# Attention start of a fused block: maxima 12 tiles ahead instead of 11, head 0 finished in front of head 1's maxima, and the stacks of the first nine heads dealt anew

## The chip, the cores and the metric

One Trainium2 chip, one core. The metric is the device time of one execution of the whole kernel in microseconds; three runs of the kernel before gave a median of 968.77 us (965.73 to 971.95).

## The reference, cut to what matters

32 heads of attention (4 batches of 8), then two gated feed-forward blocks. Only the attention part, the first third of the time, is touched.

```python
q_rot, k_rot = rotate(q), rotate(k)          # x*cos + swapped(x)*sin
scores = scale * q_rot @ k_rot.T             # 576 x 576 per head, 64 deep
scores = scores - max(scores, axis=-1)
attn = exp(scores) / (sum(exp(scores)) + 1e-9)
out = attn @ v
```

## The kernel before

Numbers are fp32, and TensorE takes a rounded form of it (fp32r); so each operand is cut into a high part and a rest, and the two are stacked in the 128 rows of one tile. **K1**, **Q1**, **K2**, **Q2** are these stacks of a head (five buffers each, so head h uses buffer h mod 5). A head has five tiles of 128 keys or queries (the last has 64).

The work of a head h goes through these stages:

- **load(h)** brings the 576 KB of q and k and of their swapped halves into `raw` (four buffers).
- **rope(h)**: three products and sums of 128 x 576 on GpSimd (POOL), for the first heads partly on VectorE (DVE).
- **stacks**: `high` is a copy on ScalarE (ACT) of the rotated rows into K1, and two copies by DMA from K1[64:] into Q1[:64] and Q2; `low` is a subtraction on POOL into K2 and two copies by DMA, K2 into Q1[64:] and K1[:64] into K1[64:]. This last one overwrites what the two copies of `high` read, so it waits for both to land. All four are issued on the queue of SyncE (SP), which is in order. `first_stacks` makes the same with ACT and DVE alone, without DMA.
- **maxima** (`row_max`, tiles `sm`): a query tile against all keys with K1 and Q1, and a DVE reduction into a column of `MX`. When the five columns of a head are there, TensorE transposes them, DVE copies them to `mt`, and a DMA on ACT's queue writes them as a row into Q2. So the subtraction of the maximum is one more row of the second pair of matmuls of `scores`.
- **scores** (tiles `st`): K1 x Q1, then K2 x Q2 with that row, then exp on ACT into `pc` (for the fifth tile `pt` and `ph`, and a subtraction on DVE).
- **values** (tiles `pv`): attn times v, 3 tiles behind the scores; the fifth tile takes `VS`, the stacks of v.

The main loop counts **ticks** t: tick t holds scores of tile t mod 5 of head t // 5. Maxima of head m, tile c are taken at tick 5m + c - AHEAD, 11 ticks ahead of that tile's scores, after a ramp at the start. Everything else is put into a table by tick (`later`), for most heads by LEAD: the rope's three steps 26, 25 and 23 ticks ahead of tick 5h, `high` 20, `low` 17, the row of -1 in K2 11. A tick is a place in the order, not a time: each engine runs its own instructions in the order in which they were written and waits for data alone. From tick 15 on, eleven chunks of weights (`raw64`, `t64`) are loaded and converted beside this, one every ten ticks, each with two operations on ACT, four on DVE and one on POOL.

The start before: `warm` matmuls on zeros while head 0 is loaded; the maxima of head 0 (tick -9) and its row (`first_row`); then the maxima of head 1 with idle matmuls between them; then tick 0.

Of the kernel before, what the change touches and what calls it, by code (L numbers as in the profile page):

```python
# [8 lines left out]
F32 = mybir.dt.float32  # L9
# [3 lines left out]
AF = mybir.ActivationFunctionType  # L13
# [29 lines left out]

INVERSE = 5, 7, 8, 11, (24, 26)

MATRIX, APART, CONVERT, ROWS = 15, 10, 15, (151, 159)


IDLE = 17, 2, 5, 0, 2, 5, 6, 1, 0, 1


@with_exitstack
def tile_kernel(ctx: ExitStack, tc: tile.TileContext, qk, vv, tabs, w_in, g_ln, wsgT, b_sg, w_out, u_r, v_r, w1, w2, out):
    nc = tc.nc
# [31 lines left out]
    D = 64  # L86
# [65 lines left out]

    def stacks(h, ticks):

        rot = RAW[h % NR][:, 0]
        K1, Q1, K2, Q2 = (t[h % NS] for t in (K1s, Q1s, K2s, Q2s))
        a, z = slice(0, D), slice(D, P)

        def high():
            nc.scalar.activation(K1, rot, AF.Copy)
            nc.sync.dma_start(f(Q1[a]), f(K1[z]))
            nc.sync.dma_start(f(Q2[a, 0:S]), f(K1[z]))

# [4 lines left out]
        if h < len(BY_ACT):  # L170
            steps = rope(nc.gpsimd, h) + first_stacks(h)
        else:
            steps = rope(nc.gpsimd, h) + (high, low, lambda: nc.sync.dma_start(f(K2[D:D + 1]), less_one))
            value_stacks(h)
        for tick, fn in zip(ticks, steps):
            later(tick, fn)

    def value_stacks(h):
        VS = VSs[h % 4]
        src = VVs[(h // 2) % 3][:, SPLIT, h % 2, :D]  # L180
        later(max(NC * h - SPLIT_V[0], SPLIT_V_FIRST[0]), lambda: nc.scalar.activation(VS[:, 0, :, :D], src, AF.Copy))
        later(max(NC * h - SPLIT_V[1], SPLIT_V_FIRST[1]), lambda: (nc.gpsimd if h > 1 else nc.vector).tensor_tensor(VS[:, 1, :, :D], src, f(VS[:, 0, :, :D]), ALU.subtract))

    def first_stacks(h):

        rot = RAW[h % NR][:, 0]
# [3 lines left out]
        def copy(on_act, out, x):  # L190
            if on_act:
                nc.scalar.activation(out, x, AF.Copy)
            else:
                nc.vector.tensor_copy(out, x)

        def high():
            e = BY_ACT[h]
            copy(e[0], Q1[z], rot[z])
            copy(e[1], Q1[a], rot[z])
            copy(e[2], K1[a], rot[a])  # L200
            copy(e[3], K1[z], rot[a])
            copy(e[4], Q2[a, 0:S], rot[z])

        def low():
            nc.vector.tensor_tensor(Q1[z], rot[z], f(Q1[z]), ALU.subtract)
            nc.vector.tensor_tensor(K2[a], rot[a], f(K1[a]), ALU.subtract)
        value_stacks(h)
        return high, low

    def row_max(h, t, done, tick):  # L210

# [25 lines left out]

# [135 lines left out]
    def later(t, fn):  # L373
        due.setdefault(t, []).append(fn)
# [24 lines left out]
    for fn in rope(nc.vector, 1)[:1] + rope(nc.gpsimd, 1)[1:]:
        later(T0, fn)  # L400
    for h in range(2):
        for tick, fn in zip(FIRST[h], first_stacks(h)):
            later(tick, fn)
# [23 lines left out]
    def warm(i):

        if i == 0:
            ps = psp.tile([P, 2, 512], F32, tag="ss", name="warm", bufs=3)[:, 0]  # L430
        elif IDLE[i]:
            ps = psp.tile([P, 2, 512], F32, tag="pv", name="warm", bufs=1)[:, 1]
        for _ in range(IDLE[i]):
            nc.tensor.matmul(ps, idle[:, :P], idle, start=True, stop=True)

    warm(0)
    n_max, last = 0, {}
    for t in range(T0, NC * NH + LAG):
        v = divmod(t - LAG, NC)
        if t >= LAG and v[1] == NC - 1:  # L440
            values(*v, t)
        if 0 <= t < NC * NH:
            if t < 3:
                warm(7 + t)
            scores(*divmod(t, NC))
        lo = lows[:-1] if 0 <= t < NC * NH and t % NC in SPLITS else lows[:]
        for fn in lo:
            fn()
        del lows[:len(lo)]
        if t >= LAG and v[1] == 0:  # L450
            values(*v, t)
        upto = 0 if t < -9 else NC if t < MAX_1 else max(2 * NC, min(t + AHEAD + 1, 2 * NC + RAMP * (t - RAMP_FROM) // 10, NC * NH))
        ready = [m for m, due_at in last.items() if due_at <= t]
        while n_max < upto or ready:
            m, c = divmod(n_max, NC) if n_max < upto else (NH, 0)
            done = ready.pop(0) if ready else None
            last.pop(done, None)
            if done == 0:
                warm(1)
                first_row()  # L460
                continue
            if m == 1:
                warm(2 + c)
# [453 lines left out]
```

## Time and profile before

| what | value |
|---|---|
| median of three runs | 968.77 us |
| the profiled execution's own time | 971.01 us |
| its span, first to last instruction | 969.2 us |
| attention, end of the last values | about 326 us |
| TensorE busy over the span | 96% |
| mean granted TensorE clock | 0.989 |

The span is the profiler's, the time is the device's for the same execution: 1.8 us lie outside the span. The median lies 2.2 us under that execution. Start and length of a row are in us; PE is TensorE, PEld its weight loads, SPq and ACTq the DMA queues of SP and ACT. A tick takes 1.7 us where TensorE never waits.

### The profile page before, as it was taken

The numbers are of one execution on the slowest core, as the hardware profiler recorded it, in microseconds if no ns is written. First come the engines' busy times: TensorE is split into PE (matmuls) and PEld (weight loads), VectorE is DVE, ScalarE is ACT, GpSimd is POOL, SyncE is SP. The second block draws the span as 40 slices with busy tenths as digits, with TensorE's granted clock in tenths as the row PEclk, the third lists the DMA queues.
The fourth block names the chain that finished last, engine by engine and source line by source line (L and its number), as shares of the span: only waits on it lengthen the run. The fifth ranks groups of instructions, "written<-read, shape, count | busy, mean of one in ns | idle before, by whom it ended". The sixth has DMA issues, their size and how long they took to land.

```text
span 969.2 us, 13195 instructions
## 1 busy us (share of the span) xinstructions
PE 930.1 (96%) x5180; PEld 783.9 (81%) x5180; DVE 534.9 (55%) x721; ACT 345.0 (36%) x550; POOL 387.9 (40%) x323
## 2 busy tenths in 40 slices
PE   6899999989989999999999899999999999999998
PEld 3587777767777798999999787888888888888887
DVE  7767878888775487443426945752652452222222
ACT  4366665556656553312315432321321230001000
POOL 7677887878751486242325542210210210000000
PEclk7899999999999999999999999999999999999999
DMA  5578677777651230000003001220230110000112
GB/s 176 141 189 207 174 176 181 192 169 190 151 139 33 72 123 1 2 1 1 23 23 109 22 22 36 95 88 1 69 106 1 57 53 0 1 1 22 44 45 86
DMA packets 58079, 78.00 MB, mean 80 GB/s; under 512 B 30505, under 2 KB 33860, under 8 KB 58018
## 3 DMA queue, kind: packets, MB, share of 16 engines
q1 hardware_dynamic: 57708, 77.08, 29.4%
q8 instruction: 41, 0.67, 0.3%
q14 instruction: 20, 0.16, 0.1%
q10 hardware_dynamic: 310, 0.08, 0.0%
HBM read 55.09 MB, written 4.79 MB: 62 GB/s over the span
## 4 chain that ended last, share of the span: by engine, by line
PE 73%; DVE 13%; DMA 9%; issue 2%; POOL 1%; ACT 1%; SPq 0%; DVEq 0%; POOLq 0%; ACTq 0%
PE a L544 20%; PE r L544 20%; PE pv L273 9%; DMA Q<-mt 6%; PE st L245 6%; PE w L544 5%; PE m L544 3%; PE sm L216 3%; PE u L544 3%; PE v L544 3%; DVE MX L221 2%; DVE ph L256 2%; DVE t L74 1%; DVE t L75 1%; DMA g<-in_wsgT 1%
## 5 line engine op out<-in xcount | busy, mean ns | idle before, releaser
L221 DVE TENSOR_REDUCE MX<-sm 128x1 f32<-128x576 f32 (+1 forms) x160 | 119.7, 751 | 58.9 <-PE sm L216 50.1
L273 PE MATMUL pv<-pc,VV 128*65 128x288 f32 x512 | 144.7, 405 | 0.5 <-DVE sums L294 0.5
L245 PE MATMUL st<-Q,K 65*128 65x288 f32 (+3 forms) x640 | 128.6, 321 | 15.6 <-DMA Q<-mt 13.9
L245 PEld LDWEIGHTS st<-Q,K 65*128 65x128 f32 (+3 forms) x640 | 96.0, 179 | 31.5 <-DMA Q<-mt 16.2
L737 DVE SCALAR_TENSOR_TENSOR RL<-r,RH 128x1024 fp32r<-128x1024 f32 (+1 forms) x38 | 42.3, 1112 | 123.8 <-ACT RH L736 123.7
L736 ACT ACTIVATE RH<-r 128x1024 fp32r<-128x1024 f32 (+1 forms) x38 | 35.6, 936 | 207.2 <-PE r L544 207.2
L248 ACT ACTIVATE pc<-st 128x576 f32<-128x576 f32 x128 | 81.8, 646 | 49.3 <-PE st L245 44.7
L752 DVE TENSOR_TENSOR X<-a,X 128x256 f32<-128x256 f32 (+4 forms) x65 | 46.4, 745 | 90.7 <-PE a L544 90.6
L544 PE MATMUL a<-RH,setB 128*128 128x512 f32 (+1 forms) x320 | 93.3, 368 | 0.0
L273 PEld LDWEIGHTS pv<-pc,VV 128*65 128x65 f32 x512 | 68.2, 137 | 29.6 <-DVE sums L294 0.7
L216 PE MATMUL sm<-K,Q 128*128 128x288 f32 (+1 forms) x320 | 77.3, 326 | 10.8 <-DVE MX L221 5.0
L544 PE MATMUL a<-RH,setA 128*128 128x512 f32 (+1 forms) x288 | 83.5, 366 | 0.0
L544 PE MATMUL r<-UH,setB 128*128 128x512 f32 (+1 forms) x256 | 73.2, 363 | 0.0
L544 PE MATMUL r<-UH,setA 128*128 128x512 f32 (+1 forms) x256 | 72.9, 363 | 0.1
L216 PEld LDWEIGHTS sm<-K,Q 128*128 128x128 f32 (+1 forms) x320 | 51.3, 184 | 20.2 <-DVE MX L221 6.3
L544 PEld LDWEIGHTS a<-RH,setB 128*128 128x128 f32 x320 | 58.2, 189 | 10.0
L148 POOL TENSOR_TENSOR raw<-raw,tab 128x576 f32<-128x576 f32 x30 | 45.9, 1530 | 43.4 <-DMA raw<-in_qk 43.4
L508 POOL TENSOR_TENSOR setB<-t,setB 128x512 fp32r<-128x512 f32 x16 | 20.7, 1295 | 102.9 <-ACT setB L697 91.8
L544 PEld LDWEIGHTS a<-RH,setA 128*128 128x128 f32 x288 | 52.1, 188 | 9.2
L544 PE MATMUL a<-RL,setB 128*128 128x512 f32 (+1 forms) x160 | 58.9, 368 | 0.0
L149 POOL TENSOR_TENSOR raw<-raw,tab 128x576 f32<-128x576 f32 x31 | 53.2, 1716 | 5.0 <-DMA raw<-in_qk 5.0
L544 PE MATMUL a<-RL,setA 128*128 128x512 f32 (+1 forms) x144 | 52.9, 368 | 0.0
(169 smaller groups left out, 1972.2 us busy)
## 6 DMA issues: line engine op xcount, KB each, us to landing
raw<-in_qk SPq DMA_DIRECT2D x31, 576.0 KB
Q<-K SPq DMA_DIRECT2D x87, 144.0 KB
raw<-in_w SPq DMA_DIRECT2D x24, 512.0 KB
VV<-in_vv SPq DMA_DIRECT2D x32, 160.0 KB
rb<-rr SPq DMA_DIRECT2D x15, 288.0 KB
K<-K SPq DMA_DIRECT2D x29, 144.0 KB
raw<-in_w_in SPq DMA_DIRECT2D x8, 512.0 KB
gt<-in_w SPq DMA_DIRECT2D x8, 512.0 KB
```

What stands on the lines that cost most here:

```text
L148: lambda: e.tensor_tensor(raw[:, 0], raw[:, 0], tab[:, 0], ALU.mult),
L149: lambda: e.tensor_tensor(raw[:, 1], raw[:, 1], tab[:, 1], ALU.mult),
L216: nc.tensor.matmul(ps[:TS[t], n, :HALF], Q1[:, t * P:t * P + TS[t]], K1[:, n * HALF:(n + 1) * HALF], start=True, stop=True)
L221: nc.vector.tensor_reduce(MXs[h % 2][:TS[t], t:t + 1], ps[:TS[t], :, :HALF], AX.XY, ALU.max)
L245: nc.tensor.matmul(ps[:kk, n, :HALF], l[:, c * P:c * P + kk], r[:, ns], start=st, stop=not st)
L248: nc.scalar.activation(h2(pc[:kk]), ps[:kk, :, :HALF], AF.Exp, scale=0.125)
L273: nc.tensor.matmul(o, l, r, start=(c == 0 and j == 0), stop=(c == NC - 1 and j == len(pr) - 1))
L508: return nc.gpsimd.tensor_tensor(out, a, b, ALU.subtract)
L544: nc.tensor.matmul(o, l, rr, start=(j == 0), stop=(j == n - 1))
L736: nc.scalar.activation(RH[:, s], ps[:, :, :WIDE[blk]], AF.Relu)
L737: nc.vector.scalar_tensor_tensor(RL[:, s], ps[:, :, :WIDE[blk]], 0.0, f(RH[:, s]), ALU.max, ALU.subtract)
L752: nc.vector.tensor_tensor(X[b][:, e2, xs], ps[:, :n, us], X[b][:, e2, xs], ALU.add)
```

## The change

- AHEAD is 12 instead of 11: in the steady part every maximum is written one tick earlier, and so is the row by its transpose and its DMA. The other steps of heads 11 to 31 keep their ticks.
- At the start, `first_head` puts head 0's row together piece by piece between its maxima. The scores of head 0 then come at once, and the maxima of head 1 between them (`MAXIMA` says how many maxima are written by each tick: 5 up to tick 1, 10 at tick 4, 15 at tick 7, 40 at tick 27). The values of head 0 are brought forward, and head 1's row is put together like head 0's at tick 5.
- Three heads instead of five get their stacks from ACT and DVE (`early_stacks`); head 2's with two copies by DMA. Heads 3 to 10 have ticks of their own (`LEADS`, six steps as in LEAD), and the loads of heads 4 to 12 (`LOADS`).
- The row's DMA of heads 2 to 5 comes one tick after the transpose's tick, which is now one after the last maximum, not two (`ROW`).
- Idle matmuls: 22 at the start instead of 17, ten of 384 columns between head 0's maxima, none later.

```diff
-LEAD_IN = (-20, -19, -19, -8, -8, 1), (-19, -18, -16, -3, -1, 4), (-3, -3, 0, 2, 4, 8)
+LEADS = {3: (4, 5, 6, 7, 8, 11), 4: (8, 9, 10, 11, 12, 15), 5: (12, 13, 14, 15, 16, 19), 6: (16, 17, 18, 19, 19, 23),
+         7: (19, 20, 21, 22, 22, 26), 8: (22, 23, 24, 25, 25, 29), 9: (25, 26, 27, 28, 29, 34), 10: (28, 29, 30, 31, 33, 39)}
+LOADS = {4: -8, 5: 3, 6: 6, 7: 8, 8: 12, 9: 16, 10: 19, 11: 22, 12: 25}
...
-AHEAD, RAMP_FROM, RAMP, MAX_1, ROW, ROW_0, ROW_1 = 11, -1, 25, -1, 2, -8, -9
+AHEAD, ROW = 12, (1, 2)
...
+        if h < 2:
+            return q + [dve(K1[a], rot[a]), act(K1[z], rot[a]), *lows, act(Q2[a, 0:S], rot[z])]
+        return q + [act(K1[a], rot[a]), send(K1[z], K1[a]), send(Q2[a, 0:S], Q1[a]), *lows]
...
+    def row_piece(h, ps, t):
+        nc.tensor.matmul(ps[:1, t // 4, t % 4 * P:(t % 4 + 1) * P], MXs[h][:, t:t + 1], ident, start=True, stop=True)
+        if t == 3:
+            nc.scalar.activation(Q2s[h][D:D + 1, :4 * P], ps[:1, 0, :4 * P], AF.Copy)
+        if t == 4:
+            nc.vector.tensor_copy(Q2s[h][D:D + 1, 4 * P:], ps[:1, 1, :P])
+
+    def first_head():
+        ps = psp.tile([P, 2, 512], F32, tag="pv", name="first_row", bufs=1)
         for t in range(NC):
+            row_max(0, t, None, 0)
+            if t > 1:
+                row_piece(0, ps, t - 2)
+            for _ in range(IDLE[1]):
+                nc.tensor.matmul(ps[:, 1, P:], idle[:, :P], idle[:, P:], start=True, stop=True)
+        for t in (NC - 2, NC - 1):
+            row_piece(0, ps, t)
...
+    early = {3: [(0, 0)], 4: [(0, 1), (0, 2)]}
...
+        if t == NC:
+            low_parts(len(lows))
+            values(0, 3, t)
+            ps = psp.tile([P, 2, 512], F32, tag="ss", name="second_row", bufs=3)
+            for c in range(NC):
+                row_piece(1, ps, c)
+            values(0, 4, t)
...
-        upto = 0 if t < -9 else NC if t < MAX_1 else max(2 * NC, min(t + AHEAD + 1, 2 * NC + RAMP * (t - RAMP_FROM) // 10, NC * NH))
+        upto = NC if t < 0 else min(MAXIMA.get(t, NC * NH), t + AHEAD + 1, NC * NH)
```

**Place 1, ACT's order, head 6.** Before, the copy that begins head 6's stacks (K1 buffer 1 from raw buffer 2) stands behind the exp of head 2's first tile; the numbers behind a name's first underscore are head or buffer, and tile:

```order
L248 ACTIVATE pc2_0_501<-st2_0_496 128x576
L162 ACTIVATE K1_1_96<-raw2_91 128x576
L248 ACTIVATE pc2_1_523<-st2_1_518 128x576
L226 DMA Q2_3_113<-mt4_509 1x5x128
L289 ACTIVATE stage1_536<-pv1_465 65x576
```

Now it stands behind the last tile of head 3, nine ticks later:

```order
L252 ACTIVATE pt3_631<-st3_4_626 64x576
L254 ACTIVATE ph3_633<-pt3_631 64x576
L182 ACTIVATE VS_1_121<-VV_2_119 128x64
L165 ACTIVATE K1_1_96<-raw2_91 128x576
L248 ACTIVATE pc4_0_664<-st4_0_659 128x576
```

So `high` of head 6 moved from tick 10 to tick 19, and `low` on POOL with it from tick 13 to tick 19.

**Place 2, TensorE's order, from the last scores of head 3 to the first maxima of head 6.** Before, the first maxima of head 6 follow head 3's last scores, nine ticks behind the copy of place 1:

```order
L245 MATMUL st3_4_663<-Q1_3_103,K1_3_98 64x288 x2
L245 MATMUL st3_4_663<-Q2_3_113,K2_3_108 64x288 x2
L216 MATMUL sm6_0_672<-K1_1_96,Q1_1_101 128x288 x2
L273 MATMUL pv3_653<-pc3_1_618,VV_1_118 65x288 x2
L245 MATMUL st4_0_686<-Q1_4_104,K1_4_99 128x288 x2
```

Now they come two ticks later, but that copy stands at the top of this piece, behind st3_4:

```order
L245 MATMUL st3_4_626<-Q2_3_113,K2_3_108 64x288 x2
L206 MATMUL sm5_2_635<-K1_0_95,Q1_0_100 128x288 x2
L206 MATMUL sm5_3_639<-K1_0_95,Q1_0_100 128x288 x2
L273 MATMUL pv3_613<-pc3_1_570,VV_1_118 65x288 x2
L245 MATMUL st4_0_659<-Q1_4_104,K1_4_99 128x288 x2
L245 MATMUL st4_0_659<-Q2_4_114,K2_4_109 128x288 x2
L206 MATMUL sm5_4_667<-K1_0_95,Q1_0_100 64x288 x2
L273 MATMUL pv3_613<-pc3_2_598,VV_1_118 65x288 x2
L245 MATMUL st4_1_675<-Q1_4_104,K1_4_99 128x288 x2
L245 MATMUL st4_1_675<-Q2_4_114,K2_4_109 128x288 x2
L206 MATMUL sm6_0_682<-K1_1_96,Q1_1_101 128x288 x2
```

Between the copy and the first use stood nine ticks of TensorE's work; nine pairs of matmuls stand there now.

**Place 3, DVE's order in the steady part, at the row of head 13** (`mt13`). Before, the row's copy stands behind the subtraction for `ph` of head 10 and one maximum:

```order
L256 TENSOR_TENSOR ph10_1368<-pt10_1366,ph10_1368 64x576
L221 TENSOR_REDUCE MX_1_116<-sm13_1_1390 128x1
L224 CAST mt13_1395<-sm13_1_1390 5x128
L221 TENSOR_REDUCE MX_1_116<-sm13_2_1412 128x1
L325 TENSOR_TENSOR X0_66<-stage4_823,rb2_1158 64x576
```

Now it stands in front of that subtraction and of the last step of a conversion:

```order
L77 SCALAR_TENSOR_TENSOR t64_175<-raw64_174,t64_175 128x512
L211 TENSOR_REDUCE MX_1_116<-sm13_1_1368 128x1
L214 CAST mt13_1373<-sm13_1_1368 5x128
L78 SCALAR_TENSOR_TENSOR t64_175<-raw64_174,t64_175 128x512
L256 TENSOR_TENSOR ph10_1366<-pt10_1364,ph10_1366 64x576
```

The row is made one tick and up to two DVE operations earlier. The row's tile is named after the head whose maxima run beside it, one more than the head it belongs to.

## Rows read from the trace of the kernel before

**Rows 1.** Page, parts 4 and 5: shares of the chain, and the scores' group.

```profile
PE a L544 20%; PE r L544 20%; PE pv L273 9%; DMA Q<-mt 6%; PE st L245 6%; PE w L544 5%; PE m L544 3%; PE sm L216 3%; PE u L544 3%; PE v L544 3%; DVE MX L221 2%; DVE ph L256 2%; DVE t L74 1%; DVE t L75 1%; DMA g<-in_wsgT 1%
L245 PE MATMUL st<-Q,K 65*128 65x288 f32 (+3 forms) x640 | 128.6, 321 | 15.6 <-DMA Q<-mt 13.9
```

**Rows 2.** Busy time by stage: stretch, length, PE, PEld, DVE, ACT, POOL, clock, DMA share.

```profile
45.60:103.00 57.40, 57.37 (x343) 46.17 (x343) 40.99 (x55) 36.63 (x65) 42.56 (x38) 1.00 0.74 195
103.00:275.00 172.00, 156.64 (x914) 122.71 (x914) 141.25 (x192) 100.27 (x181) 137.11 (x109) 1.00 0.74 177
```

**Rows 3.** Timeline of the start: start, length, engine, line, operation.

```profile
7.57 0.76 DVE L150 TENSOR_TENSOR raw<-raw 128x576 f32<-128x576 f32 x1
...
14.30 3.40 DVE L221 TENSOR_REDUCE MX<-sm 128x1 f32<-128x576 f32 x5
...
17.31 2.29 PE L232 MATMUL first_row<-ident,MX 128*1 128x128 f32 x10
...
22.90 1.25 DVE L194 CAST Q<-raw 64x576 fp32r<-64x576 f32 x1
...
26.05 1.83 DVE L206 TENSOR_TENSOR K<-raw,K 64x576 fp32r<-64x576 f32 x1
...
40.89 0.91 PE L245 MATMUL st<-Q,K 128*128 128x288 f32 x4
```

**Rows 4.** Timeline: one head's stacks, copy, two DMAs, subtraction, last DMA.

```profile
37.49 0.67 ACT L162 ACTIVATE K<-raw 128x576 fp32r<-128x576 f32 x1
38.70 0.59 SPq L164 DMA_DIRECT2D Q<-K  x1
41.24 0.46 SPq L169 DMA_DIRECT2D K<-K  x1
```

**Rows 5.** Chain of waits, ticks 10 to 28: start, length, what.

```profile
50.21 0.53 PE st L245 x4
50.74 0.27 PE sm L216 x2
...
51.12 0.97 PE pv L273 x4
...
61.39 1.50 PE pv L273 x8
...
80.68 0.52 PE st L245 x4
```

**Rows 6.** Granted clock (third from the right) in two stretches of the start.

```profile
20.60:27.40 6.80, 3.15 (x16) 1.54 (x14) 6.64 (x6) 2.82 (x6) 6.67 (x4) 0.98 0.48 121
27.40:34.20 6.80, 5.60 (x19) 3.50 (x19) 4.58 (x7) 0.23 (x1) 5.52 (x4) 0.52 0.51 139
```

**Rows 7.** Timeline of SP's queue in the steady part.

```profile
130.59 0.49 SPq L169 DMA_DIRECT2D K<-K  x1
...
132.25 0.39 SPq L137 DMA_DIRECT2D raw<-in_qk  x1
...
133.31 0.54 SPq L164 DMA_DIRECT2D Q<-K  x1
...
140.31 0.46 SPq L169 DMA_DIRECT2D K<-K  x1
```

**Rows 8.** Waits of 100 to 280 on SP's queue: total, times, longest.

```profile
SPq L169 <- DMA Q<-K: 41.7, 21, 3.8
```

**Rows 9.** Timeline of ACT, then chain of waits, from head 12's row on.

```profile
128.71 0.68 ACT L254 ACTIVATE ph<-pt 64x576 fp32r<-64x576 f32 x1
129.30 0.24 ACT L181 ACTIVATE VS<-VV 128x64 fp32r<-128x64 f32 x1
129.75 0.65 ACT L248 ACTIVATE pc<-st 128x576 f32<-128x576 f32 x1 [0.21 <-PE st L245]
...
132.96 7.05 DMA Q<-mt
...
146.52 0.28 PE sm L216 x2
```

More of the change, by code (lines that the diff above doesn't have):

```diff
@@ L33 @@
 LEAD = 26, 25, 23, 20, 17, 11
-LEAD_IN = (-20, -19, -19, -8, -8, 1), (-19, -18, -16, -3, -1, 4), (-3, -3, 0, 2, 4, 8)
-FIRST = (-17, -10), (-9, -9)
-BY_ACT = (0, 1, 1, 1, 1), (1, 1, 0, 1, 1), (1, 0, 1, 1, 1)
-LOAD, LOAD_V, SPLIT_V, SPLIT_V_FIRST = 30, 11, (6, 1), (-11, -1)
-AHEAD, RAMP_FROM, RAMP, MAX_1, ROW, ROW_0, ROW_1 = 11, -1, 25, -1, 2, -8, -9
+LEADS = {3: (4, 5, 6, 7, 8, 11), 4: (8, 9, 10, 11, 12, 15), 5: (12, 13, 14, 15, 16, 19), 6: (16, 17, 18, 19, 19, 23),
+         7: (19, 20, 21, 22, 22, 26), 8: (22, 23, 24, 25, 25, 29), 9: (25, 26, 27, 28, 29, 34), 10: (28, 29, 30, 31, 33, 39)}
+LOADS = {4: -8, 5: 3, 6: 6, 7: 8, 8: 12, 9: 16, 10: 19, 11: 22, 12: 25}
+MAXIMA = {0: 5, 1: 5, 2: 7, 3: 9, 4: 10, 5: 11, 6: 13, 7: 15, 8: 15, 9: 15, 10: 16, 11: 18, 12: 20, 13: 20, 14: 21, 15: 23,
+          16: 25, 17: 25, 18: 27, 19: 29, 20: 30, 21: 31, 22: 33, 23: 35, 24: 36, 25: 38, 26: 39}
+EARLY = 3
+LOAD, LOAD_V, SPLIT_V, SPLIT_V_FIRST = 31, 11, (6, 1), {0: (1, 1), 1: (4, 4)}
+AHEAD, ROW = 12, (1, 2)
 INVERSE = 5, 7, 8, 11, (24, 26)
 MATRIX, APART, CONVERT, ROWS = 15, 10, 15, (151, 159)
-IDLE = 17, 2, 5, 0, 2, 5, 6, 1, 0, 1
+IDLE = 22, 2
 @with_exitstack
@@ L169, in low @@
             nc.sync.dma_start(f(K1[z]), f(K1[a]))
[L170 to L174, printed above, removed]
+        steps = rope(nc.gpsimd, h) + (high, low, lambda: nc.sync.dma_start(f(K2[D:D + 1]), less_one))
+        value_stacks(h)
         for tick, fn in zip(ticks, steps):
@@ L180, in value_stacks, with early_stacks @@
         src = VVs[(h // 2) % 3][:, SPLIT, h % 2, :D]
-        later(max(NC * h - SPLIT_V[0], SPLIT_V_FIRST[0]), lambda: nc.scalar.activation(VS[:, 0, :, :D], src, AF.Copy))
-        later(max(NC * h - SPLIT_V[1], SPLIT_V_FIRST[1]), lambda: (nc.gpsimd if h > 1 else nc.vector).tensor_tensor(VS[:, 1, :, :D], src, f(VS[:, 0, :, :D]), ALU.subtract))
-    def first_stacks(h):
+        at = SPLIT_V_FIRST.get(h) or [NC * h - o for o in SPLIT_V]
+        later(at[0], lambda: nc.scalar.activation(VS[:, 0, :, :D], src, AF.Copy))
+        later(at[1], lambda: nc.gpsimd.tensor_tensor(VS[:, 1, :, :D], src, f(VS[:, 0, :, :D]), ALU.subtract))
+    def early_stacks(h):
         rot = RAW[h % NR][:, 0]
@@ L188, in first_stacks @@
         a, z = slice(0, D), slice(D, P)
[L190 to L208, printed above, removed]
+        act = lambda out, x: lambda: nc.scalar.activation(out, x, AF.Copy)
+        dve = lambda out, x: lambda: nc.vector.tensor_copy(out, x)
+        low = lambda out, x, hi: lambda: nc.vector.tensor_tensor(out, x, f(hi), ALU.subtract)
+        send = lambda out, x: lambda: nc.sync.dma_start(f(out), f(x))
+        q = [act(Q1[z], rot[z]), dve(Q1[a], rot[z])]
+        lows = [low(Q1[z], rot[z], Q1[z]), low(K2[a], rot[a], K1[a])]
+        if h < 2:
+            return q + [dve(K1[a], rot[a]), act(K1[z], rot[a]), *lows, act(Q2[a, 0:S], rot[z])]
+        return q + [act(K1[a], rot[a]), send(K1[z], K1[a]), send(Q2[a, 0:S], Q1[a]), *lows]
     def row_max(h, t, done, tick):
@@ L226, in row_max @@
             later(tick + 1, lambda: nc.scalar.dma_start(row, f(mt)))
-    def first_row():
-        ps = psp.tile([P, 2, 512], F32, tag="ss", name="first_row", bufs=3)
-        for t in range(NC):
-            nc.tensor.matmul(ps[:1, t // 4, t % 4 * P:(t % 4 + 1) * P], MXs[0][:, t:t + 1], ident, start=True, stop=True)
-        nc.scalar.activation(Q2s[0][D:D + 1, :4 * P], ps[:1, 0, :4 * P], AF.Copy)
-        nc.vector.tensor_copy(Q2s[0][D:D + 1, 4 * P:], ps[:1, 1, :P])
+    def row_piece(h, ps, t):
[6 more added lines that the diff above has]
+        ps = psp.tile([P, 2, 512], F32, tag="pv", name="first_row", bufs=1)
+        for t in range(NC):
+            row_max(0, t, None, 0)
[5 more added lines that the diff above has]
+            row_piece(0, ps, t)
     PVS, PCS = {}, {}
@@ L382, in tile_kernel @@
         nc.sync.dma_start(RAW[0][:, x], qk[0, 0, x])
-    for h in range(1, NR):
+    load(1)
+    load_v(0)
+    for h in range(2, NR):
         load(h)
-    for i in range(2):
-        load_v(i)
-    for i in range(len(BY_ACT)):
+    load_v(1)
+    for i in range(EARLY):
         nc.gpsimd.memset(f(K2s[i][D:D + 1]), -1.0)
@@ L390, in tile_kernel @@
         nc.gpsimd.memset(VVs[i][:, :, :, D:], 1.0)
-    for i in range(2):
-        nc.gpsimd.memset(MXs[i], 0.0)
+    nc.gpsimd.memset(MXs[0], 0.0)
     for i in range(4):
@@ L396, in tile_kernel @@
     nc.sync.dma_start(less_one, f(K2s[0][D:D + 1]))
-    for fn in rope(nc.vector, 0):
+    for fn in rope(nc.vector, 0) + tuple(early_stacks(0)):
         fn()
[L399 to L403, printed above, removed]
+    nc.vector.memset(MXs[1], 0.0)
+    nc.gpsimd.memset(MXs[1], 0.0)
+    for fn in rope(nc.gpsimd, 1):
+        fn()
+    for h in range(EARLY):
+        value_stacks(h)
+    for tick, fn in zip((-8, -8, -8, -8, -8, 3, 3), early_stacks(1)):
+        later(tick, fn)
+    for fn in rope(nc.gpsimd, 2):
+        later(1, fn)
+    for fn in early_stacks(2):
+        later(4, fn)
     for i in range(2, NP):
         later(2 * NC * i - LOAD_V, lambda i=i: load_v(i))
-    for h in range(2, NH):
-        stacks(h, LEAD_IN[h - 2] if h < 5 else [NC * h - o for o in LEAD])
+    for h in range(EARLY, NH):
+        stacks(h, LEADS.get(h) or [NC * h - o for o in LEAD])
     for h in range(NR, NH):
-        later(NC * h - LOAD - (h > 2 * NR), lambda h=h: load(h))
+        later(LOADS.get(h, NC * h - LOAD), lambda h=h: load(h))
     WTICK = [MATRIX + APART * i for i in range(2 * KT + 3)]
@@ L425, in tile_kernel, with low_parts @@
         later(ROWS[1] + 2 * k, lambda k=k: x_lo(0, k))
[L427 to L437, printed above, removed]
+    ps = psp.tile([P, 2, 512], F32, tag="ss", name="warm", bufs=3)[:, 0]
+    for _ in range(IDLE[0]):
+        nc.tensor.matmul(ps, idle[:, :P], idle, start=True, stop=True)
+    def low_parts(n):
+        for fn in lows[:n]:
+            fn()
+        del lows[:n]
+    early = {3: [(0, 0)], 4: [(0, 1), (0, 2)]}
+    n_max, last = NC, {}
     for t in range(T0, NC * NH + LAG):
         v = divmod(t - LAG, NC)
-        if t >= LAG and v[1] == NC - 1:
+        if t == -9:
+            first_head()
+        if t == NC:
[5 more added lines that the diff above has]
+            values(0, 4, t)
+        if v[0] > 0 and v[1] == NC - 1:
             values(*v, t)
         if 0 <= t < NC * NH:
-            if t < 3:
-                warm(7 + t)
             scores(*divmod(t, NC))
[L446 to L450, printed above, removed]
+        low_parts(len(lows) - (0 <= t < NC * NH and t % NC in SPLITS))
+        if v[0] > 0 and v[1] == 0:
             values(*v, t)
-        upto = 0 if t < -9 else NC if t < MAX_1 else max(2 * NC, min(t + AHEAD + 1, 2 * NC + RAMP * (t - RAMP_FROM) // 10, NC * NH))
+        upto = NC if t < 0 else min(MAXIMA.get(t, NC * NH), t + AHEAD + 1, NC * NH)
         ready = [m for m, due_at in last.items() if due_at <= t]
@@ L457, in tile_kernel @@
             last.pop(done, None)
[L458 to L463, printed above, removed]
             row_max(m, c, done, t)
@@ L466, in tile_kernel @@
                 n_max += 1
-                if c == NC - 1:
-                    last[m] = t + ROW if m > 1 else ROW_1 if m else ROW_0
-        if t >= LAG and 0 < v[1] < NC - 1:
+                if c == NC - 1 and m > 1:
+                    last[m] = t + ROW[m > 5]
+        if v[0] > 0 and 0 < v[1] < NC - 1:
             values(*v, t)
+        for e in early.get(t, ()):
+            values(*e, t)
         for fn in due.pop(t, []):
```

## The prediction

> **What bounds the kernel now.** I read the page first. TensorE leads the chain, but the row's DMA, Q<-mt, holds 6% of it, and the scores waited 13.9 us for it [rows 1]. The table by stage says where: from 45.6 to 103 TensorE is never idle; from 103 to 275, where weights are converted, it is idle for 172.00 - 156.64 = 15.4 us at a full clock [rows 2]. The timeline of the start is the second place: head 1's first scores end only at 41.8 [rows 3], and DVE, not TensorE, is what leads there. From then on a head costs five scores of 0.53, five maxima of 0.27, three values of 0.97 and the last two for 1.50 together, 8.4 to 8.5 us or 1.7 a tick [rows 5]; ticks 10 to 28 take 80.68 - 50.21 = 30.5.
>
> For the steady part the queue of SP is the view to read. Each head's last copy (L169) waits for the copies behind the raw load to land: 41.7 us in 21 waits [rows 8]. From one L169 to the next 140.31 - 130.59 = 9.7 us go by, longer than a head's 8.5: 1.7 until the raw load is issued, 1.1 until L164 is, 7.0 until that has landed [rows 7]. Nothing of this waits for TensorE. So the supply of K1 seems to run at some 9.7 us a head there, and the wait for the row is where TensorE meets that pace: head 12's row is issued 0.7 us behind the raw load of 132.25 and takes 7.05 [rows 7, 9].
>
> The Trainium skill (DMA: Bandwidth & Descriptors, "Queues, rings and completion order") says that a DMA's semaphore counts up only after every earlier write of that DMA engine, across its queues. By that rule 2.5 KB behind a raw load is as late as the load, which the 7.05 bears out; and a row issued ahead of the load would be free of it; if that freed TensorE of all 13.9 us, the sum would be rival 1's.
>
> **The start, up to tick 10.** Against the order before, DVE loses one product of head 1 (0.76) and gets one more cast (1.25) ahead of head 0's maxima, which end at 14.30 + 3.40 = 17.7 now [rows 3] and so at about 18.2. The last piece of the row takes a fifth of 2.29, the copy some 0.3: head 0's row is there at 19.0, and its scores follow. Head 1 has nothing yet by then. For it DVE does two casts and a subtraction, while POOL waits for ACT, so I take the uncontended 0.76 of 128 x 576 for each: 21.3. Four maxima, paced by TensorE's three PSUM buffers: 24.6. A subtraction of K2 beside POOL's rope 1.83, the last maximum 0.7: 27.2. Then come, ahead of `ph` of head 0, the cast and two subtractions of head 2, 1.25 + 1.83 + 1.83, `ph` itself 0.8, and head 1's row 0.3 [rows 3]: 33.2. TensorE can do nothing after the row's pieces at 28.5 until the last value of head 0 gets its `ph`. So head 1's first scores end at about 34.2 instead of 41.8 (bounds 32.5 and 36).
>
> Five ticks with little of values take 5 x 0.80 + 2 x 0.97 = 6 us [rows 5]; the pause of 4.7 may cost clock, as now a stretch in which TensorE was idle for 3.65 of 6.8 us is followed by one at 0.52 instead of 0.98 [rows 6], for which I add 1. Then the row of head 2: its DMA stands on ACT behind the last exp, `ph` and VS of head 1, 0.65 + 0.68 + 0.24 [rows 9], and has 2.5 us to land (the nearest row: a copy issued at 38.70 let L169 go at 41.24 [rows 4]). So the scores of tick 10 end at 44.7 instead of 50.7: **6.0 us ahead**, with 15 maxima done where before there were 21, so that up to tick 28 seven more have to be made: 7 x 0.27 = 1.9.
>
> **Ticks 10 to 28.** Here the change puts ACT's copy, two pairs of DMAs in series and the first maxima of the same head 2 to 4 ticks apart, where 9 lay between. From the start of that copy at 37.49 L169 goes out at 41.24 [rows 4], 3.75 later, and lands another 2.5 after that if it takes what the copy before took: 6.25. Where a raw load stands in front, L164 alone took 7.0 [rows 7]: about 10.8. I take 6.7, close to the quiet end, because these loads are issued behind the copies of the head before. TensorE's own work in between, from the scores that the copy stands behind, and the exp of 0.65:
> - head 4: 5.2 us against 7.35, waits 2.1; heads 5 and 8: 6.2 against 7.35, 1.15 each;
> - head 6: two pairs of scores, three maxima, two values, 3.8, against 7.35 and `ph` and VS 0.92, waits 4.45;
> - head 7: 3.1 against 7.35, waits 4.25.
>
> Head 3's row is issued on ACT, at some 53.4 by the same count, right behind head 8's raw load. Between the 2.5 of a free transfer and the 7.0 behind a load I take 4.4, and TensorE comes at 55.4: 2.4 (0 to 4). Sum 15.5; with the quiet 6.25 and no wait for the row 10.9; with the loaded 10.8 over 30. POOL sets a floor of its own: five ropes of three operations and five subtractions between head 3 and head 8.
>
> So tick 28 comes 15.5 + 1.9 - 6.0 = **11.4 us later** than now. The quiet end with the start's own lower bound gives 5; above I stop at 20, since every wait also lets the transfers behind it drain.
>
> **The steady part.** The row is made a tick earlier, and in front of two DVE operations instead of behind them, and should go out ahead of the raw load, so the ten waits for it mostly end. What is late next is K1 and Q1 for the maxima, also a tick earlier: the L169 of 140.31 lands at 142.8 by the same 2.5, and that head's first maxima come after the last ones of the head before, at 146.52 [rows 9], so near 147. Of these 4 us a tick takes 1.7; TensorE can gain the rest, 2.1 to 2.5 (I take **2.1**), before it waits for the copies at SP's pace. The loads of heads 11 and 12 come 2 and 4 ticks earlier, so that the slow pace begins later: **2** (0 to 3). Idle matmuls lie in pauses: nothing. Values brought forward: nothing by themselves.
>
> **Sum:** +11.4 - 2.1 - 2.0 = +7.3 against the profiled 971.0, that is 978.3 there; the median was 2.2 lower, so **976** from 968.8.
>
> **Rivals.**
> 1. *SP's pace was TensorE's.* If SP only looks independent, and follows once the row is early, the whole 13.9 comes back instead of 2.1: 976 - 11.8 = 964. For it: from 45.6 to 103 the same loads kept up with 8.5 a head [rows 2]. Against it: 41.7 us of waits in which TensorE has no part [rows 8].
> 2. *The copies of heads 4 to 8 come in time*, since TensorE or DVE is slower there than I count: then 1.9 - 6.0 = -4.1, and with the 4.1 above 961. Against it: head 7's 3.1 us of work lies under even the quiet 6.25. With rival 1 as well: 949.
> 3. *The pauses cost clock.* The waits of over 4 us at heads 6 and 7, and the one at 28.5, each bring a stretch like 27.40 to 34.20 at 0.52, in which real matmuls take twice as long: up to 3.4 us each, some 10 in all: 986. [...] The Trainium skill (TensorE: Matmul & The Clock Gate, "Part 1: The HAM clock gate") says the same, that an engine found idle is put at half its rate.
>
> **How the numbers follow.** A measurement of this kernel tells about 1% (9.7 us) from no change. Forecast 50%, own range 969 to 983; rival 1 18%, rival 2 12%, both 5%, rival 3 15%. Faster by over 1% (under 959) needs both of the first two, or more than I count of one: 0.13. Slower by over 1% (over 978.5) is rival 3 and the upper third of the forecast: 0.32. The rest, 0.55. The range 957 to 986 leaves out "both" and the end of rival 3.
>
> **What will show it.** Head 0's scores near 19, tick 10's near 44; then on TensorE waits for Q<-K or K<-K in front of the first maxima of heads 4 to 8, of 3 to 5 us at heads 6 and 7. Between 110 and 280 few waits for Q<-mt, waits for the copies at the maxima instead, and still about 9.6 us a head. Wrong if those waits are not there, or if the steady part runs at 8.5 us a head. The stages behind the attention should move as a block.

## The result, and the profile after

The changed kernel takes 980.18 us (median of 4 runs, 979.8 to 988.11) against 967.63 (4 runs) before: ratio 1.0136, 95% interval 1.0103 to 1.0169, so slower by 1.4%. That lies in the range of 957 to 986, 4.2 above the forecast of 976.0. The profiled execution of after took 988.11 (span 986.1), some 8 above the median, so its trace places the loss better than it sizes it (sizes that are read from it are rough).

The page of after, part 5, three groups of instructions (busy, mean ns, then idle time before them and what ended most of it):

```profile
L245 PE MATMUL st<-Q,K 65*128 65x288 f32 (+3 forms) x640 | 128.7, 325 | 3.4 <-DMA Q<-mt 2.2
...
L206 PE MATMUL sm<-K,Q 128*128 128x288 f32 (+1 forms) x320 | 77.2, 329 | 28.2 <-DMA K<-K 13.2
...
L170 POOL TENSOR_TENSOR K<-raw,K 128x576 fp32r<-128x576 f32 x29 | 42.8, 1477 | 28.3 <-ACT K L165 27.4
```

The change did what it says: the scores' waits for their row went from 13.9 [rows 1] to 2.2 us. In their place the maxima wait, 28.2 us in all against 10.8 before, most plainly for the last copy of their head's stacks; and GpSimd waited 27.4 us, against 5.9 before, for ScalarE's copy of the same stacks.

The table by stage of after, in the two stretches of [rows 2]:

```profile
45.60:103.00 57.40, 44.83 (x238) 34.48 (x237) 27.84 (x40) 23.62 (x41) 37.71 (x32) 0.91 0.62 150
103.00:275.00 172.00, 158.86 (x921) 124.78 (x921) 141.20 (x190) 103.05 (x185) 138.47 (x110) 0.99 0.75 176
```

The stretch in which TensorE was never idle now has 57.40 - 44.83 = 12.6 us of idle time, at a lower mean clock. In the steady stretch TensorE is busy for 158.86 - 156.64 = 2.2 us more, of the 15.4 that stood idle, part of it at the lower clock (0.99).

Timeline of TensorE in after, against [rows 3, 5]: the last value of head 0, then head 1's first scores, the second half of tick 10's, and the scores of ticks 28 and 50; then tick 50 in the timeline of before:

```profile
31.91 0.72 PE L273 MATMUL pv<-ph,VS 128*65 128x288 f32 x4 [3.73 <-DVE ph L256]
32.47 0.93 PE L245 MATMUL st<-Q,K 128*128 128x288 f32 x4
...
42.47 0.53 PE L245 MATMUL st<-Q,K 65*128 65x288 f32 x2 [1.46 <-DMA Q<-mt]
...
91.98 0.70 PE L245 MATMUL st<-Q,K 128*128 128x288 f32 x4
...
134.10 0.90 PE L245 MATMUL st<-Q,K 128*128 128x288 f32 x4
```

```profile
119.44 0.64 PE L245 MATMUL st<-Q,K 128*128 128x288 f32 x2
```

Head 1's first scores end at 33.4, 8.4 us ahead of before; tick 10's at 43.0, 7.7 ahead. Tick 28 stands at 91.98 instead of 80.68, **11.3 behind**: 19 us are lost in 18 ticks. Tick 50 is 14.7 behind.

The 19 us, by the table by stretch from the end of tick 10's scores to tick 28, before and after:

```profile
50.74:80.68 29.94, 29.94 (x182) 24.24 (x182) 19.24 (x26) 18.18 (x32) 23.74 (x22) 1.00 0.73 196
```

```profile
43.00:91.98 48.98, 37.94 (x195) 29.14 (x195) 21.64 (x32) 18.58 (x33) 28.18 (x24) 0.90 0.60 149
```

TensorE stands idle for 48.98 - 37.94 = 11.0 us, where it was never idle before, and its matmuls take 37.94 - 29.94 = 8.0 us longer: seven more maxima, 1.9 by the count of the prediction, and the rest, about 6, with a granted clock of 0.90 instead of 1.00.

How one of those losses comes about, in the chain of waits of after, heads 5 and 6:

```profile
57.21 2.68 DMA Q<-K
...
59.95 4.43 DMA K<-K
...
64.52 1.30 PE sm L206 x4
...
66.87 0.65 ACT pt L252
...
68.38 0.58 ACT K L165
...
69.53 2.48 DMA Q<-K
...
72.08 2.25 DMA K<-K
...
74.42 0.50 PE sm L206 x2
```

The last copy of head 5 holds the maxima until 64.52. Behind these maxima stand the scores, behind the scores ScalarE's exp, behind the exp its copy of head 6, then GpSimd's subtraction and two pairs of DMAs in series, and these hold the maxima of head 6 until 74.42. **Each late copy makes the next one late.** The same stretch from GpSimd's side, in its timeline:

```profile
61.32 1.39 POOL L153 TENSOR_TENSOR raw<-raw 128x576 f32<-128x576 f32 x1
...
69.03 1.41 POOL L170 TENSOR_TENSOR K<-raw,K 128x576 fp32r<-128x576 f32 x1 [6.04 <-ACT K L165]
```

Head 6 was rotated at 62.71; its copy needed nothing more, and yet stood on ScalarE behind an exp until 68.3.

### The profile page after: what moved, and what is told of

The parts are those of the page before. It is cut to its first block, busy times and chain, and to the rows that moved or that the text cites. A ratio compares the mean times of both kernels' runs of the same rounds, so it can differ in the third digit from the quotient of the medians.

```text
span 986.1 us, 13203 instructions
## 1 busy us (share of the span) xinstructions
PE 937.0 (95%) x5182; PEld 789.6 (80%) x5182; DVE 521.6 (53%) x721; ACT 343.2 (35%) x547; POOL 385.3 (39%) x326
## 4 chain that ended last, share of the span: by engine, by line
PE 72%; DMA 11%; DVE 8%; ACT 3%; POOL 3%; issue 2%; SPq 1%; ACTq 1%; POOLq 0%; DVEq 0%
PE a L551 20%; PE r L551 20%; PE pv L273 7%; PE w L551 5%; PE st L245 5%; PE m L551 4%; PE v L551 4%; DMA rr<-rc 4%; DMA Q<-K 3%; PE sm L206 3%; PE u L551 3%; DVE MX L211 1%; DMA K<-K 1%; DMA g<-in_wsgT 1%; ACT pc L248 1%
## 5 line engine op out<-in xcount | busy, mean ns | idle before, releaser
L273 PE MATMUL pv<-pc,VV 128*65 128x288 f32 x512 | 148.1, 414 | 0.8 <-DVE sums L294 0.5
L206 PE MATMUL sm<-K,Q 128*128 128x288 f32 (+1 forms) x320 | 77.2, 329 | 28.2 <-DMA K<-K 13.2
L151 POOL TENSOR_TENSOR raw<-raw,tab 128x576 f32<-128x576 f32 x31 | 45.3, 1461 | 37.6 <-DMA raw<-in_qk 37.4
L170 POOL TENSOR_TENSOR K<-raw,K 128x576 fp32r<-128x576 f32 x29 | 42.8, 1477 | 28.3 <-ACT K L165 27.4
```

Source lines behind the costliest of these rows:

```text
L206: nc.tensor.matmul(ps[:TS[t], n, :HALF], Q1[:, t * P:t * P + TS[t]], K1[:, n * HALF:(n + 1) * HALF], start=True, stop=True)
```

## The experiments

The theory has two halves. **Start:** the new order puts the stacks of heads 4 to 8 two to four ticks ahead of their first use, so that nothing hides their latency; that costs more than the early scores bring. **Steady part:** the order on SP closes a loop that sets some 9.7 us a head, whatever the distance of the maxima. Rival 1 is that the distance gives back all the row waits, rival 3 that the clock is the loss. All runs stand against fresh runs of the kernel before (967.75, 969.78 and 969.11 in the three sets).

**1. The distance alone: after with 11, before with 12.**

```diff
-AHEAD, ROW = 12, (1, 2)
+AHEAD, ROW = 11, (1, 2)
```

> The changed kernel, with its maxima 11 tiles ahead again from tick 27 on and its own start kept: the steady part as before, the start as changed. Against the kernel before. Main theory (the start costs some 14 us, the distance of 12 gives back only some 2 because the copies on SP set the pace): 981 to 984, and the waits of scores for the row come back (8 to 14 us) while those of maxima for copies shrink by about as much. Rival 1 (the distance of 12 gives back all that the rows cost, some 12): 990 to 994. Rival 3 (the distance costs something itself): below 979.

982.51, ratio 1.0143 [1.0117, 1.0169]: 2.3 above after's median, too little to be told from it. The scores' waits for their row came back, 9.2 us in all (8 to 14 expected), and the maxima no longer wait behind 100 us. In the other kernel:

```diff
-AHEAD, RAMP_FROM, ... = 11, -1, ...
+AHEAD, RAMP_FROM, ... = 12, -1, ...
```

> The kernel before with its maxima 12 tiles ahead, nothing else changed: its own start. Main theory: 964 to 967, with the row waits of 13.9 us nearly gone and 8 to 12 us of waits of maxima for copies in their place. Rival 1 (TensorE sets the pace, the row waits come back as time): 953 to 958. Rival 3: 968 or more.

966.76, ratio 0.9981 [0.9956, 1.0006]. What the distance does there is seen in the waits from 100 to 320 us on TensorE, SP's queue and GpSimd (total, times, longest):

```profile
PE sm L216 <- ACT pc L248: 8.4, 7, 2.2
PE sm L216 <- DMA K<-K: 4.3, 3, 2.2
...
SPq L169 <- DMA Q<-K: 47.5, 23, 3.7
...
POOL raw L148 <- DMA raw<-in_qk: 38.3, 18, 5.1
```

No wait for a row is left; 8.4 + 4.3 us of waits of maxima stand in its place, and SP's and GpSimd's waits for DMAs go on. (ScalarE, named in the first row, frees a PSUM buffer. In the runs of part 3, which open the loop, these waits are gone too, so they belong with the copies.) Rival 1's 11.8 is excluded from both sides: the distance of 12 is worth 1.0 here and 2.3 there by the medians, and neither is clear of noise.

**2. The start of after: the order of the copies, and the clock.** ScalarE's copy and GpSimd's subtraction of heads 4 to 8 one tick earlier:

```diff
-4: (8, 9, 10, 11, 12, 15), 5: (12, 13, 14, 15, 16, 19), ...
+4: (8, 9, 10, 10, 11, 15), 5: (12, 13, 14, 14, 15, 19), ...
```

> The changed kernel with the copy on ScalarE and the subtraction on GpSimd of heads 4 to 8 one tick earlier in the order, nothing else. Main theory (the pauses of 1.8 to 3.2 us at the first maxima of heads 5 to 8 are waits for copies that are ordered too late on ScalarE): these pauses fall to under 1 us each, the clock stays at its upper level from 60 to 100 us, and the whole comes to 968 to 974. Rival (the copies are paced by the raw loads and the DMA queues, and an earlier order only moves the wait): 977 to 981.

976.6, ratio 1.0080 [1.0054, 1.0107]: between what the theory and the rival expected. Tick 28 came at 86.15, 5.8 earlier, but two pauses were left, 1.9 and 3.3 us, at the first maxima of heads 6 and 7. The chain of waits of this run says why:

```profile
60.77 5.32 DMA Q<-K
...
70.12 5.16 DMA Q<-K
```

and SP's timeline has, ahead of the first of these:

```profile
58.54 0.44 SPq L140 DMA_DIRECT2D raw<-in_qk  x1
...
60.77 0.60 SPq L167 DMA_DIRECT2D Q<-K  x1
...
66.13 0.46 SPq L172 DMA_DIRECT2D K<-K  x1
```

Brought forward by a tick, the copies (L167) stand right behind a raw load and take 5.3 and 5.2 instead of the 2.7 and 2.5 that such copies took in after. Order and queue both count.

Idle matmuls in front of the first maxima of heads 5 to 8:

```diff
+            for _ in range(HOLD.get(h, 0) if t == 0 else 0):
+                nc.tensor.matmul(ps[:, 1, HALF:], idle[:, :P], idle[:, HALF:], start=True, stop=True)
```

> The changed kernel with 30, 12, 26 and 14 idle matmuls in front of the first maxima of heads 5, 6, 7 and 8, so that TensorE doesn't stand still there; the copies come as late as before. Main theory (some 9 us of the loss are the waits themselves, some 4 to 5 the lower clock after them): 975 to 978, no 1.2 GHz stretch between 60 and 100 us. Rival 3 in its strong form (most of the loss is clock): below 973. Rival (the clock costs nothing there): 980 or more.

981.63, ratio 1.0124 [1.0092, 1.0156]: nothing returned. In after, the table by stretch shows the pause at head 5 and, behind it, a granted clock of 0.50, which is 1.2 GHz:

```profile
60.70:64.50 3.80, 0.90 (x4) 0.28 (x3) 0.00 (x0) 0.61 (x1) 2.13 (x4) 0.86 1.01 258
64.50:70.30 5.80, 5.47 (x17) 4.18 (x18) 3.99 (x6) 2.05 (x4) 1.27 (x1) 0.50 0.34 76
```

With the idle matmuls, the same stretch of that run, and the one behind it:

```profile
60.00:70.00 10.00, 8.74 (x64) 7.12 (x63) 3.61 (x7) 3.87 (x7) 3.84 (x6) 1.00 0.72 172
70.00:80.00 10.00, 8.14 (x46) 6.80 (x45) 4.25 (x6) 3.17 (x5) 5.78 (x5) 0.83 0.49 118
```

The clock stayed up behind heads 5 and 7 (1.00 from 80 to 90 us too); behind a pause of 1.9 us at head 6 it fell, so the expected "no 1.2 GHz stretch" came only in part: the mean from tick 10's scores to tick 28 rose from 0.90 to 0.97. Tick 28 came at 92.29 all the same, against 91.98. Head 5's first maxima came at 66.1 there, 1.6 later than in after, again behind its last copy, so a microsecond or two of clock can't be ruled out. Rival 3's 10 can: 0.90 over the 48.98 us of after is at most 4.9 us of work at a full clock.

**3. The loop on SP, in the kernel before with 12 tiles.** First only where the raw loads stand, behind the two copies that follow ScalarE's:

```diff
-        later(NC * h - LOAD - (h > 2 * NR), lambda h=h: load(h))
+        later(NC * h - (35 if h > 2 * NR else LOAD), lambda h=h: load(h))
```

> The kernel before with its maxima 12 tiles ahead, and each raw load from head 9 on 35 tiles ahead of its head instead of 31, so that on SP's queue it stands behind the two copies that follow the copy on ScalarE, and in front of the two that wait for GpSimd's subtraction. Main theory (SP's order closes a loop of two heads: load, rotation on GpSimd, subtraction of the head ahead, SP's wait of 2 to 4 us with its last copy, next load; that sets the 9.7 us per head): the loop opens, the waits of SP with the last copy fall below 15 us, those of GpSimd for raw loads below 10, and the whole comes to 955 to 960. Rival A (the DMA queues' throughput sets the pace, their share is 0.75): 965 to 969. Rival B (GpSimd's or ScalarE's own work sets it): 965 to 969 too, with GpSimd without idle time.

**950.45**, ratio 0.9798 [0.9771, 0.9826]: better than expected, and the lowest median here of a kernel that does all the work. From 100 to 320 us SP's waits with L169 for Q<-K fell from 47.5 to 0.4, and GpSimd's for raw loads from 38.3 to nothing. SP's timeline with 12 tiles and the loads at their old place:

```profile
150.22 0.49 SPq L169 DMA_DIRECT2D K<-K  x1
...
151.93 0.40 SPq L137 DMA_DIRECT2D raw<-in_qk  x1
152.45 0.47 SPq L163 DMA_DIRECT2D Q<-K  x1
153.01 0.54 SPq L164 DMA_DIRECT2D Q<-K  x1
...
157.65 0.46 SPq L168 DMA_DIRECT2D Q<-K  x1
161.00 0.46 SPq L169 DMA_DIRECT2D K<-K  x1
```

and with the loads at the new one:

```profile
153.78 0.51 SPq L163 DMA_DIRECT2D Q<-K  x1
...
154.98 0.58 SPq L137 DMA_DIRECT2D raw<-in_qk  x1
...
157.81 0.49 SPq L168 DMA_DIRECT2D Q<-K  x1
158.40 0.54 SPq L169 DMA_DIRECT2D K<-K  x1
```

In the first, L169 follows L168 by 3.35 us, since it overwrites what L163 and L164 still read behind the raw load; the next raw load follows L169, GpSimd rotates when that has landed, its subtraction of the head before waits in line, and L168 waits for the subtraction. In the second, L169 follows at once. The table by stage of this run:

```profile
103.00:275.00 172.00, 172.00 (x1033) 139.65 (x1032) 153.47 (x212) 113.33 (x203) 143.76 (x117) 1.00 0.72 187
```

TensorE is never idle. In this stretch the DMA engines moved 187 GB/s, against 176 with the loads at the old place, so their throughput was not the limit there (rival A); nor was the work of GpSimd or ScalarE, which is the same in both (rival B). The run moves the load four ticks forward and behind the two copies at once, and can't tell the one from the other.

Second, the same wait removed in another way, the loads where they were:

```diff
-            nc.sync.dma_start(f(Q1[a]), f(K1[z]))
-            nc.sync.dma_start(f(Q2[a, 0:S]), f(K1[z]))
+            nc.scalar.activation(Q1[a], rot[z], AF.Copy)
+            nc.sync.dma_start(f(Q2[a, 0:S]), f(Q1[a]))
```

> The kernel before with its maxima 12 tiles ahead, and in the steady stacks the copy of the upper half into Q1 made by ScalarE (one more copy of some 0.65 us per head) instead of by a DMA out of K1; the second one's DMA reads Q1. So the last copy on SP has no DMA in front of it to wait for. Main theory (SP's loop): SP's waits with the last copy for Q<-K end, one turn of two heads gets some 2 to 4 us shorter, and the whole comes to 956 to 961. Rival A (throughput of the DMA queues): 964 to 968, from the one DMA less per head. Rival B (ScalarE's work): 969 or more.

957.18, ratio 0.9861 [0.9836, 0.9886]. Its waits from 100 to 320:

```profile
SPq L168 <- POOL K L167: 40.9, 9, 4.8
...
POOL raw L148 <- DMA raw<-in_qk: 8.4, 8, 1.8
```

SP no longer waits with L169, and GpSimd's waits for raw loads fell from 38.3 to 8.4; the rest of the chain, through the subtraction, is still there. Third, the raw loads of heads 12 and on left out:

> The kernel before with its maxima 12 tiles ahead, and the raw loads of heads 12 and on left out (the heads are computed on what the buffers hold). Main theory and rival A alike: no waits of GpSimd for raw loads, TensorE's waits in heads 12 to 30 under 3 us in all, 953 to 958. Rival B (the work of GpSimd or ScalarE sets the pace): 963 or more.

949.75, ratio 0.9790 [0.9765, 0.9814]. Without the loads, with heads computed on whatever the buffers hold, it is no faster than with them in the right place.

Last, the distance of 11 as before, and only the load order changed:

> The kernel before with its maxima 11 tiles ahead as they were, and each raw load from head 9 on 35 tiles ahead of its head. Main theory (the row waits too were a late symptom of the same loop: the row's DMA stood behind a raw load that had slipped): 950 to 955, row waits under 4 us in all. Rival 1 in its part (the distance of 12 is needed to hide the row): 958 to 964, with row waits of 8 us or more.

951.51, ratio 0.9803 [0.9772, 0.9833]: the row waits, too, are gone. They were a symptom of the same order, and with it mended the distance of the maxima is worth 1 us or nothing. The Trainium skill (DMA: Bandwidth & Descriptors, "Queues, rings and completion order") has the rule for the row: a semaphore counts up only behind every earlier write of its DMA engine. It agrees with 13.9 us of row waits where the row stood behind a load, and none where the loads stand elsewhere; no run here tests it by itself.

**4. What the start costs.** After with its raw loads from head 13 on moved in the same way, its start kept:

```diff
-LOAD, LOAD_V, ... = 31, 11, ...
+LOAD, LOAD_V, ... = 35, 11, ...
```

> The changed kernel with its raw loads from head 13 on 35 tiles ahead instead of 31 (behind the copies that follow the copy on ScalarE); its start is kept. Main theory (the loop through SP is open now, so what is left against the kernel before with the same load order and 12 tiles, 950.45, is the cost of the new start): 962 to 967, 12 to 16 above that run, with the pauses at the first maxima of heads 5 to 8 as in the changed kernel and no waits of maxima behind 130 us. Rival (the late stacks of the start are made up for once the loop is open): 952 to 957. Rival C (the change's loss lies behind the start): 972 or more.

966.47, ratio 0.9961 [0.9941, 0.9982]: 16.0 above the kernel before with the same distance and, from head 13 on, the same loads. That is the new start with its own loads, by itself. Then its stacks ordered earlier:

```diff
-LEADS = {3: (4, 5, 6, 7, 8, 11), ... 5: (12, 13, 14, 15, 16, 19), 6: (16, 17, 18, 19, 19, 23), ...
+LEADS = {3: (4, 4, 4, 5, 5, 11), ... 5: (10, 11, 12, 13, 13, 19), 6: (14, 15, 15, 16, 16, 23), ...
-LOADS = {... 7: 8, 8: 12, 9: 16, 10: 19, 11: 22, 12: 25}
+LOADS = {... 7: 9, 8: 13, 9: 16, 10: 20, 11: 23, 12: 27}
-MAXIMA = {... 5: 11, 6: 13, ... 9: 15, 10: 16, 11: 18, ...
+MAXIMA = {... 5: 12, 6: 15, ... 9: 16, 10: 18, 11: 20, ...
```

> The changed kernel with its stacks of heads 3 to 10 dealt one to three ticks earlier (copy and subtraction in one tick, as soon as GpSimd can have rotated), raw loads of heads 7 to 12 behind the copies that follow ScalarE's, from head 13 on 35 tiles ahead, and the maxima of heads 2 and 3 made one tick earlier for their rows. Main theory (the loss of the start is the late dealing of the stacks, not the earlier scores): most of the start's 12 to 16 come back and a few more from head 1's scores that stand 8 us earlier: 945 to 953. Rival (the copies' length under load sets the start, wherever they are dealt): 957 to 963. Rival (GpSimd's own work, 6 us per head, is too long for the start): 957 or more, with GpSimd without idle time from 35 to 90 us.

952.09, ratio 0.9818 [0.9788, 0.9848]: 14.4 of the 16.0 are back, with head 0's and head 1's early scores kept. The run moves copies, loads and a few maxima together, so it shows that the order of the start is the loss, and not what each part of it costs. In TensorE's timeline of this run tick 28 stands 3.6 ahead of [rows 5]:

```profile
77.11 0.69 PE L245 MATMUL st<-Q,K 128*128 128x288 f32 x4
```

Both changes at once, the copies of heads 4 to 8 a tick earlier and ScalarE's second copy:

> The changed kernel with copy and subtraction of heads 4 to 8 one tick earlier, and the copy into Q1 made by ScalarE as in the run beside it. Main theory: the copies of heads 5 to 8 land some 2 to 3 us sooner after the subtraction, the two pauses of 1.9 and 3.3 us at the first maxima of heads 5 and 6 shrink to under 1 us, and the steady part gains as in the run beside it: 962 to 968. Rival A: 974 to 977. Rival B: 977 or more.

962.05, ratio 0.9916 [0.9893, 0.9939], tick 28 at 81.98; the two pauses are gone but for 0.3 us, as expected of it (they stood at heads 6 and 7; the expectation counts them as 5 and 6); the longest wait from tick 10 on is one of 3.9 us for a row.

## Why the prediction was right, and where it was not

*The start up to tick 10.* Right: head 1's first scores end at 33.4, forecast 34.2; tick 10's at 43.0, forecast 44.7, so 7.7 ahead and not 6.0.

*Ticks 10 to 28.* The mechanism was right: TensorE waits for the copies at the first maxima of heads 4 to 8, and the run with earlier stacks gives most of it back. That the sum came out right, 11.3 later against a forecast of 11.4, is luck. The start was 1.7 better than forecast. The pauses at the maxima of heads 4 to 7 were 1.1, 2.9, 1.8 and 3.2, forecast 2.1, 1.15, 4.45 and 4.25; head 3's row took 0.7, forecast 2.4; all idle time in these ticks is 11.0, where 15.5 was forecast (1.15 of it for head 8, whose pause came behind tick 28). The matmuls made up for both: about 6 us more than counted, at a granted clock of 0.90, with low stretches behind heads 5 and 7 that are no term of the sum. I priced each head by itself. The trace shows that one late copy orders the next, and the run with copies a tick earlier bears that out.

*The steady part.* The main reason held: the distance of 12 is worth 2.3 and 1.0 us by the medians, forecast 2.1, and the row waits turned into waits for copies. My picture of SP's pace was half of it: L164 behind a raw load, with nothing of TensorE's in it, is the part I saw; that the raw load itself waits for L169, and L169, by way of GpSimd's subtraction, for the raw load before, and that moving it opens the loop, I did not.

*The step that failed* is "the loads of heads 11 and 12 come 2 and 4 ticks earlier, so that the slow pace begins later: 2", and with it that nothing but gains was counted behind tick 28. The table by stretch from tick 28 to tick 40, before, after, and in the run with all stacks ordered earlier, whose tick 40 comes at 101.30:

```profile
80.68:100.82 20.14, 20.14 (x123) 16.15 (x122) 16.51 (x23) 13.28 (x24) 14.23 (x13) 1.00 0.77 199
```

```profile
91.98:117.11 25.13, 21.50 (x125) 16.24 (x124) 19.98 (x24) 14.37 (x26) 24.64 (x21) 1.00 0.77 179
```

```profile
77.11:101.30 24.19, 21.55 (x126) 16.30 (x124) 19.18 (x24) 14.03 (x26) 22.55 (x19) 1.00 0.86 212
```

After loses 25.13 - 20.14 = 5.0 us here, at a full clock; head 8's pause of 2.1 lies there. From tick 40 to tick 50 it gains 1.6 (134.10 - 117.11 = 17.0 against 119.44 - 100.82 = 18.6), but the kernel before with 12 tiles gains 1.3 there by the distance alone (17.3). So the early loads brought 0.3 and not 2.

What the 5.0 are is seen in the column of GpSimd, the last before the clock: 13 operations and 14.23 us in these ticks before, 21 operations and 24.64 of 25.13 us in after, 22.55 of 24.19 in the run with earlier stacks, which has no pause at copies and still loses 4.1. Work that stood in earlier ticks before has come here, more than twelve ticks of 1.7 us hold. The prediction names this floor ("POOL sets a floor of its own") and gives it no number. How it reaches TensorE, in the timelines of the last of these runs:

```profile
83.84 1.42 POOL L153 TENSOR_TENSOR raw<-raw 128x576 f32<-128x576 f32 x1
```

```profile
85.29 0.68 ACT L165 ACTIVATE K<-raw 128x576 fp32r<-128x576 f32 x1 [3.16 <-DMA Q<-K]
```

```profile
87.12 0.80 PE L245 MATMUL st<-Q,K 128*128 128x288 f32 x4 [1.37 <-ACT pc L248]
```

GpSimd ends head 10's rotation at 85.26, and ScalarE's copy of it starts then, after 3.16 us without work (the row names a DMA that landed at the same moment); the exp stands behind that copy, and TensorE waits 1.37 us, its longest wait in these ticks. Another 1.0 it waits for `ph`, whose subtraction on DVE took 1.84 us beside GpSimd, where it took 0.75 in the kernel before with mended loads:

```profile
93.88 1.84 DVE L256 TENSOR_TENSOR ph<-pt,ph 64x576 fp32r<-64x576 f32 x1
```

```profile
93.59 0.75 DVE L256 TENSOR_TENSOR ph<-pt,ph 64x576 fp32r<-64x576 f32 x1
```

This is read from the traces; no run changes GpSimd's work by itself.

*Rivals.* Rival 1 fell with the first pair, rival 2 with the pauses seen. Rival 3 came true in part: behind heads 5 and 7 the clock fell, after pauses of 2.9 and 3.2 us, shorter than the over 4 us it spoke of; its price did not, since the run with less of the low clock was no faster.

In sum, by the runs: after with 11 tiles differs from before by the start alone, and is 14.8 us above it (13.8 by the ratio); 16.0 is the same where the loop is open. With -1.0 to -2.3 for the distance that is +11.5 to +13.8, and +12.6 was measured by the medians, +13.2 by the ratio. Forecast were +9.4 for the start with its loads and -2.1 for the distance. So what lies between +7.3 and the measured time is the start, 4.4 to 5.4 dearer than counted; the trace puts that into ticks 28 to 40 and into the gain of 2 that was not there. I had put 0.55 on "within 1%" and 0.32 on slower, which it was.

## What to carry to other kernels

Where one engine's steps are ordered by hand, price the latency of a chain that crosses engines against the distance to its first use, and look whether its first step stands behind work that waits for its last: then each delay is handed on. Count also what the engine off the critical path has to do in the ticks into which work is moved. A wait that moves when it is removed, and leaves the pace as it was, can be the end of a loop; look on the queue that everything passes through for the transfer that is ordered in front of small ones, and move that. Here one number on the raw loads was worth 2%, and the distance of the maxima, with which the change began, 0.1 to 0.2%, not clear of noise.

## What the runs showed of the hardware

Where a 576 KB load stands on SP's queue sets the latency of the 144 KB copies behind it: 2.5 to 2.7 us in after without it, 5.2 to 5.3 behind it with copies one tick earlier, at the same total traffic. Idle matmuls held the granted clock at 1.00 at two pauses that otherwise ended in 0.50 to 0.52, without any gain. The subtraction for `ph` on DVE, of two inputs in SBUF, took 0.75 us wherever GpSimd stood idle, and 0.75 to 2.0 beside a busy GpSimd, in the traces of before, of after and of three of the other runs alike. The Trainium skill (GPSIMD Engine Reference, Specifications) says that GpSimd shares its SBUF interfaces with VectorE, in contention with instructions of two SBUF inputs. These times agree with it.
